# First batch of a split-weight two-layer kernel: the first layer in quarters instead of halves, with the weight decode put in the order of the quarters

## The chip, the cores and the metric

One core of one Trainium2 chip runs the kernel. The metric is device time in microseconds of one execution; three runs of the kernel before gave a median of 1534.24 us (1533.52 to 1536.03).

## What is computed

A packed attention (32 learned queries `p` per head attend to 576 keys, then the 576 queries attend to the 32 packed rows), then two feed-forward layers, all in float32; the weights come as float64 and are read as pairs of 32-bit words.

```python
def sm_attn(qq, kk, vv):
    s = scale * np.matmul(qq, kk.transpose(0, 1, 3, 2))
    a = np.exp(s - np.max(s, axis=-1, keepdims=True))
    return np.matmul(a / (np.sum(a, axis=-1, keepdims=True) + 1e-09), vv)
...
p_packed = sm_attn(p, k, v)                  # batch 8, heads 8, seq 576, head_dim 64, 32 packed rows
out = sm_attn(q, p_packed, p_packed)         # becomes x, 4608 tokens x 512
...
h = x @ w_in;  sp = log1p(exp(h));  x = (h * tanh(sp)) @ w_out     # layer 1, d_ff 2048
h = x @ w_in2; x = (h - tanh(h)) @ w_out2                          # layer 2, d_ff 2048
```

## The kernel before

All work is written down as operations with an engine, an estimated duration, dependences, buffers to take and give, and a **key**. `Plan.emit` walks a model of the machine and, whenever an engine is free, emits the ready operation with the lowest key whose buffers are free. So the keys set the order of each engine's queue; the queues then run in that order on the chip. `ka(n)` (L285) is the planned time of round `n` of layer 1.

**Layer 1** has 128 rounds `n` (`layer1`, L627): batch `b = n // 16`, half `hf` of its tokens (288 of 576), and pair `pr` of 128-wide feature columns. A round does on PE 12 matmuls of the first product (L641: two columns, two contractions, three high/low passes), on ACT two Mish (L645) and a rounding copy (L647), on DVE the low part (L648), and on PE 24 matmuls of the second product (L659) into four PSUM accumulators `acc`, which are evacuated when all 16 columns are summed (L670). In a batch the order is half 0 with pairs 0 to 7, then half 1 with pairs 0 to 7. So the first half of batch 0 needs every weight of layer 1.

**The weight decode.** `dec_unit` (L295) loads 512 KB of words into one of four buffers `st`, and builds float32 from them: on ACT a scale (L311) and for some units a second one (L314), on DVE otherwise L316, and always L318 and L321. The 16 units of the input weights, `w1i`, go to `xw` and `x` buffers (L356), are used by `mix` and stored to DRAM as `w1i_d` for the later batches (L365). The 16 units of the output weights, `w1o`, go through one scratch buffer `rr` (L326) and are split into high and low parts in `wo[i]` by ACT (L332) and DVE (L334). `unit_key` (L346) sets their order: four of `w1i`, four of `w1o`, and so on, all ahead of or within the first eight rounds.

**Attention** of a batch (`attention`, L441): scores (L479), maxima (L485), exponentials (L494), transposes (L506, L508), the packed product (L527, L535, L537); then for each half the second scores (L553) and a softmax on DVE and ACT (L558 to L580) that ends in `a2[b, hf]`, the input of L641. The exponential and Mish are in different ACT tables, and each change of table is an ACT_TABLE_LOAD. `mix` (L591) multiplies the packed rows into four `w1i` units (L609, evacuated by L615 and L617); four of them serve a batch. All loads and stores stand in SP's queue (L292). The second layer's weights are decoded in the same way during layer 1 (`dec_pair`, L370), and layer 2 (`pair2`, L740) follows. The `x` pool has ten buffers, shared by the loads of attention and the decode.

Of the kernel before, what the change touches and what calls it, by code (L numbers as in the profile page):

```python
# [21 lines left out]
HALF = S // 2  # L22
# [48 lines left out]
class Plan:  # L71
# [24 lines left out]
    def emit(self):  # L96
# [5 lines left out]
        table = None  # L102
# [111 lines left out]
def tile_packed_attention_mish_tanhshrink(  # L214
# [80 lines left out]
    def dec_unit(src, key, out, take, on_act, split=False, after=()):  # L295
# [6 lines left out]
        ld = dma(lambda: st.tile, lambda: src.bitcast(U32), 512, key - 10, take=[st])  # L302
# [7 lines left out]

        a = op("ACT", a_cost(512), lambda: A.activation(  # L311
# [8 lines left out]
        lds.append(ld)  # L320
# [4 lines left out]
    def dec_split(src, key, buf, view, on_act, scratch=False):  # L325
        w = Buf(K["rr"], [128, 512]) if scratch else buf  # L326
# [24 lines left out]
    unit = 0  # L351
    for g in range(4):
        for i in range(4 * g, 4 * g + 4):
            key = unit_key(unit)
            unit += 1
            buf = Buf(K["xw" if i < 6 else "x"], [128, 512 if i < 6 else 576])  # L356
            wt[0, i] = (buf, dec_unit(w1i[i], key, lambda b=buf: b.tile[:, :512], [buf], i >= 5))
        for i in range(4 * g, 4 * g + 4):
            key = unit_key(unit)
            unit += 1  # L360
            wo[i] = Buf(K["wo"], [128, 2, 512])
            wo_rd[i] = dec_split(w1o[i], key, wo[i], v_oc, True, True)
    for i in range(16):
        late = lds[min(31, 30 + i)]
        wt_st[i] = dma(lambda i=i: w1i_d[i], lambda b=wt[0, i][0]: b.tile[:, :512], 256, -46.8 + i,  # L365
                       [wt[0, i][1], late], give=[wt[0, i][0]])
# [74 lines left out]
    def attention(b):  # L441
# [15 lines left out]
        def load(src, n, kb_, key):  # L457
# [8 lines left out]
                   (k0 + 0.5 * (spans[0][1] - spans[0][0]) if b else -80.7) + i) for i in range(5)]  # L466
# [4 lines left out]
        def scores(j):  # L471
# [11 lines left out]
            s1 = op("PE", 1.19, f, key(2), [pt_ld] + [x[1] for x in kk], sc + [a1], [pt] + [x[0] for x in kk])  # L483
# [12 lines left out]
            ex = [op("ACT", 2 * a_cost(HALF, True, True) + 0.5, fe, key(2), [m], [sm] if j == 0 else [],  # L496
# [43 lines left out]
        def second_scores(hf):  # L540
            k0 = key()
            qq = [load(qT[b, i, :, hf * HALF:(hf + 1) * HALF], (128, HALF), 144, (k0 if b or hf else -57.94) + i)
# [48 lines left out]
    def mix(b, g):  # L591
        k0 = ka(16 * (b - 1) + 10 + 2 * g) if b else unit_key(8 * g + 3) - 52.37
# [3 lines left out]
        for c in range(4):  # L596
            i = 4 * g + c
            if b == 0:
                ws.append(wt[0, i])
            else:  # L600
                buf = Buf(K["xw"], [128, 512])
                ws.append((buf, dma(lambda buf=buf: buf.tile[:, :512], lambda i=i: w1i_d[i], 256,
                                    k0 - 12, [wt_st[i]], [buf])))
        pm = [bank(K["cap_s"]), bank(K["cap_s"])]

        def f():
            for j in range(2):
# [19 lines left out]
    def layer1(n):  # L627
        b, hf, pr = n // 16, n // 8 % 2, n % 8
        k0 = ka(n)
        kf = k0 - 4.87  # L630
        e, gt = Buf(K["e"], [128, 2, HALF]), Buf(K["g"], [128, 2, 2, HALF])
# [18 lines left out]
        for c in range(2):  # L650
            fc = 2 * pr + c
            for oc in range(4):
                if fc == 0:
# [3 lines left out]
                def f(c=c, oc=oc, fc=fc, ac=ac):  # L657
                    for i, (wl, gl) in enumerate(PASSES):
                        T.matmul(ac.tile[:, :HALF], r(wo[fc].tile[:, wl, oc * 128:(oc + 1) * 128]),  # L659
                                 r(gt.tile[:, gl, c, :]), start=(fc == 0 and i == 0), stop=(fc == NFC - 1 and i == 2))  # L660
# [250 lines left out]
```

## Time and profile before

| | us |
|---|---|
| median of three runs | 1534.24 |
| the profiled execution, device time | 1539.05 |
| its span, first to last instruction | 1536.9 |
| PE busy | 1494.9 |
| DVE busy | 1039.5 |
| ACT busy | 1007.6 |
| DMA, mean over the span | 189 GB/s |

The page gives busy time by engine, the span in 40 slices, the chain of work that ended last, and groups of instructions by source line. Views of the trace used below: the timeline (start, duration, what ended the idle time before), busy time by stretch (with the granted TensorE clock), and the chain.

### The profile page before, as it was taken

What the parts mean: (1) busy time and instruction counts of PE and PEld (TensorE: products, weight loads), DVE (VectorE), ACT (ScalarE), POOL (GpSimd) and SP (SyncE); (2) the same over time, 40 slices, a digit from 0 to 9 for tenths busy, and PEclk for the clock granted to TensorE, in tenths of its full rate; (3) what the DMA queues carried; (4) which work ended last, traced back from release to release, by engine and by line L of the source; (5) the groups of instructions that cost most, each with busy time, mean ns of one, the idle gap of its engine ahead of it and who ended that gap; (6) DMA issues with size and microseconds to landing.
All of it is one profiled execution on the core that took longest, in us unless ns stands there. A gap on an engine that the chain in (4) does not pass through costs nothing.

```text
span 1536.9 us, 28140 instructions
## 1 busy us (share of the span) xinstructions
PE 1494.9 (97%) x11112; PEld 1342.6 (87%) x11112; DVE 1039.5 (68%) x1905; ACT 1007.6 (66%) x1995; POOL 0.2 (0%) x4
## 2 busy tenths in 40 slices
PE   5599999999999999999999999999999999999999
PEld 1398989899898989899989898989989898989887
DVE  5955574563756543241378879897888889798876
ACT  5867765665666654553477767676776767676765
POOL 0000000000000000000000000000000000000000
PEclk9799999999999999999999999999999999999999
DMA  8676674481856443120975656566566656565561
GB/s 284 209 265 208 225 237 173 157 298 59 291 181 223 136 148 102 55 71 30 333 244 173 224 185 226 169 205 208 196 200 202 208 172 223 182 228 169 186 197 57
DMA packets 100084, 289.73 MB, mean 189 GB/s; under 512 B 10224, under 2 KB 27760, under 8 KB 90736
## 3 DMA queue, kind: packets, MB, share of 16 engines
q1 hardware_dynamic: 99952, 287.94, 56.0%
q8 instruction: 87, 1.43, 0.4%
q14 instruction: 45, 0.37, 0.1%
HBM read 241.76 MB, written 46.14 MB: 187 GB/s over the span
## 4 chain that ended last, share of the span: by engine, by line
PE 95%; DMA 2%; DVE 1%; ACT 1%; SPq 0%; issue 0%; DVEq 0%
PE acc L659 27%; PE acc L827 26%; PE bk L761 23%; PE bk L641 13%; PE bk L609 2%; PE bk L479 1%; PE bk L527 1%; PE bk L553 1%; DMA x<-in_v 1%; DMA m<-w2i_d 1%; DMA st<-in_w1o 0%; PE bk L506 0%; DMA x<-in_q 0%; DMA x<-in_k 0%; ACT st L311 0%
## 5 line engine op out<-in xcount | busy, mean ns | idle before, releaser
L827 PE MATMUL acc<-g,wo 128*128 128x512 f32 x1728 | 444.2, 393 | 0.0
L659 PE MATMUL acc<-g,wo 128*128 128x288 f32 x3072 | 438.2, 297 | 0.0
L659 PEld LDWEIGHTS acc<-g,wo 128*128 128x128 f32 x3072 | 416.1, 189 | 17.2 <-issue 16.6
L827 PEld LDWEIGHTS acc<-g,wo 128*128 128x128 f32 x1728 | 306.7, 189 | 50.1
L761 PEld LDWEIGHTS bk<-yh,m 128*128 128x128 f32 x2160 | 291.9, 191 | 20.7 <-DVE x L775 2.7
L761 PE MATMUL bk<-yh,m 128*128 128x256 f32 x2160 | 306.2, 284 | 0.1
L648 DVE TENSOR_TENSOR g<-e,g 128x576 fp32r<-128x576 f32 x128 | 96.7, 755 | 220.2 <-ACT g L647 214.0
L641 PEld LDWEIGHTS bk<-a,m 128*128 128x128 f32 x1536 | 212.4, 190 | 30.8 <-issue 8.4
L641 PE MATMUL bk<-a,m 128*128 128x288 f32 x1536 | 231.3, 300 | 5.9 <-ACT a L579 4.3
L645 ACT ACTIVATE e<-bk 128x288 f32<-128x288 f32 x256 | 103.3, 411 | 150.4 <-PE bk L641 149.5
L812 DVE TENSOR_TENSOR tt<-x,tt 128x512 f32<-128x512 f32 x144 | 99.3, 690 | 69.6 <-ACT tt L805 69.5
L801 ACT ACTIVATE e<-x 128x512 f32<-128x512 f32 x144 | 90.7, 630 | 70.6 <-DVE x L775 69.2
L772 ACT ACTIVATE pc<-bk 128x256 f32<-128x256 f32 x216 | 75.6, 374 | 70.0 <-PE bk L761 68.8
L761 PEld LDWEIGHTS bk<-a,m 128*128 128x128 f32 x864 | 113.3, 191 | 8.9 <-DMA m<-w2i_d 3.0
L761 PE MATMUL bk<-a,m 128*128 128x256 f32 x864 | 115.5, 283 | 2.8 <-DMA m<-w2i_d 2.8
L806 DVE SCALAR_TENSOR_TENSOR xw<-xw,xw 128x512 f32<-128x512 f32 x144 | 99.4, 690 | 26.0 <-ACT xw L804 24.3
L814 DVE COPY_PREDICATED xw<-e,tt 128x512 f32<-128x512 uint32 x144 | 109.6, 761 | 1.6
L775 DVE TENSOR_TENSOR x<-bk,pc 128x256 f32<-128x256 f32 x216 | 89.9, 417 | 23.3 <-PE bk L761 23.0
L816 ACT ACTIVATE g<-xw 128x512 fp32r<-128x512 f32 x144 | 89.3, 620 | 22.9 <-DVE xw L814 22.4
L817 DVE TENSOR_TENSOR g<-xw,g 128x512 fp32r<-128x512 f32 x144 | 98.8, 686 | 6.9 <-ACT g L816 6.8
L802 ACT ACTIVATE xw<-e,c_qb 128x512 f32<-128x512 f32 x144 | 102.2, 710 | 0.0
L810 DVE SCALAR_TENSOR_TENSOR xw<-xw,x 128x512 f32<-128x512 f32 x144 | 98.6, 685 | 0.0
(94 smaller groups left out, 1264.1 us busy)
## 6 DMA issues: line engine op xcount, KB each, us to landing
m<-w2i_d SPq DMA_DIRECT2D x72, 1024.0 KB, 5.1
m<-w2i_d SPq DMA_DIRECT2D x72, 768.0 KB, 4.4
xw<-w1i_d SPq DMA_DIRECT2D x112, 256.0 KB, 4.3
w2i_d<-x SPq DMA_DIRECT2D x56, 256.0 KB, 3.7
x<-in_k SPq DMA_DIRECT2D x32, 288.0 KB, 4.8
x<-in_q SPq DMA_DIRECT2D x64, 144.0 KB, 4.0
y_d<-yv SPq DMA_DIRECT2D x16, 576.0 KB, 3.9
out_t<-x SPq DMA_DIRECT2D x36, 256.0 KB, 5.1
```

The lines of the kernel that those rows point to most:

```text
L641: T.matmul(h.tile[:, :HALF], r(m.tile[:, fc % 4, kc, wl, :]), r(x.tile[:, kc, al, :]), start=(i == 0), stop=(i == 5))
L645: fr.append(op("ACT", a_cost(HALF, True), lambda c=c, h=h: A.activation(e.tile[:, c, :], h.tile[:, :HALF], AF.Mish), kf + 1, [g1] + fr, [e ...
L648: lo = op("DVE", v_cost(576), lambda: V.tensor_tensor(out=r(gt.tile[:, 1]), in0=e.tile, in1=gt.tile[:, 0], op=ALU.subtract), kf + 1.2, [hi ...
L659: T.matmul(ac.tile[:, :HALF], r(wo[fc].tile[:, wl, oc * 128:(oc + 1) * 128]), r(gt.tile[:, gl, c, :]), start=(fc == 0 and i == 0), stop=(f ...
L761: T.matmul(bk.tile[:, :HB], r(wv[:, kc, wl, :]), r(yq[blk, j].tile[:, kc, yl, :]), start=(first and i == 0), stop=(i == 5), skip_group_che ...
L802: p1 = op("ACT", a_cost(TB, False, True), lambda: A.activation(s1.tile, zz.tile, AF.Sigmoid, bias=c_qb, scale=Q_L), k0 + 0.1, [sq], [s1])
L806: q = op("DVE", v_cost(TB), lambda: V.scalar_tensor_tensor(out=s1.tile, in0=s1.tile, scalar=Q_E, in1=s2.tile, op0=ALU.add, op1=ALU.mult), ...
L810: q = op("DVE", v_cost(TB), lambda: V.scalar_tensor_tensor(out=s1.tile, in0=s1.tile, scalar=Q_A, in1=h.tile, op0=ALU.mult, op1=ALU.mult), ...
L812: d = op("DVE", v_cost(TB), lambda: V.tensor_tensor(out=tt.tile, in0=h.tile, in1=tt.tile, op=ALU.subtract), k0 + 1.3, [th], give=[h])
L814: q = op("DVE", v_cost(TB), lambda: V.copy_predicated(s1.tile, zz.tile.bitcast(U32), tt.tile), k0 + 1.4, [q, d, k], give=[zz, tt])
L817: lo = op("DVE", v_cost(TB), lambda: V.tensor_tensor(out=r(gt.tile[:, 1, :]), in0=s1.tile, in1=gt.tile[:, 0, :], op=ALU.subtract), k0 + 2. ...
L827: T.matmul(ac.tile, r(w2c[fc].tile[:, wl, oc * 128:(oc + 1) * 128]), r(gt.tile[:, gl, :]), start=(fc == 0 and i == 0), stop=(fc == NFC - 1 ...
```

## The change

Batch 0 goes through layer 1 in four quarters: half 0 with pairs 0 to 3, half 1 with pairs 0 to 3, half 0 with pairs 4 to 7, half 1 with pairs 4 to 7 (`place`). The sums of the first two quarters are copied from PSUM by ACT into `part` (two `x` buffers a half), and DVE adds them to the sums of the other two quarters, in place of ACT's last copy. The decode keys follow the quarters (`w1i_key`, `w1o_key`), `w1o` uses two scratch buffers in turn (`rr` and the second layer's `so`), four `w1i` units are decoded into `wo` buffers, the first four `w1i` loads and the values `v` are issued early, and the second scores' `q` loads and the attention of batch 1 get other keys. The buffer of the first exponentials is taken by the exponential and no longer by the scores. Batches 1 to 7 and layer 2 keep their order.

```diff
-    def dec_split(src, key, buf, view, on_act, scratch=False):
-        w = Buf(K["rr"], [128, 512]) if scratch else buf
+    def dec_split(src, key, buf, view, on_act, scratch=None):
+        w = Buf(K[scratch], [128, 512]) if scratch else buf
...
-    def unit_key(u):
-        i = u // 8 * 4 + u % 4
-        return -83.7 + 3.72 * i if u % 8 < 4 else -79.34 + 6.62 * i
+    def place(hf, pr):
+        return pr // 4 * 8 + hf * 4 + pr % 4
+
+    def w1i_key(i):
+        return ka(place(0, i // 4 * 2)) - 7.0 - 1.2 * (4 - i % 4) - (0 if i < 4 else 6.0)
+
+    def w1o_key(i):
+        return ka(place(0, i // 2) + 2) - 9.0 + 3.0 * (i % 2) - (0 if i < 8 else 6.0)
...
+        kd = "wo" if 4 <= i < 8 else "x" if i > 13 else "xw"
...
+        wt[0, i] = (buf, dec_unit(w1i[i], key, wv, [buf], i % 4 > 1, early=-190.5 + i if i < 4 else None), wv)
+        wo[i] = Buf(K["wo"], [128, 2, 512])
+        wo_rd[i] = dec_split(w1o[i], w1o_key(i), wo[i], v_oc, True, "rr" if i % 2 == 0 else "so")
...
-        wt_st[i] = dma(lambda i=i: w1i_d[i], lambda b=wt[0, i][0]: b.tile[:, :512], 256, -46.8 + i,
+        wt_st[i] = dma(lambda i=i: w1i_d[i], wv, 256, w1i_key(i) + 25, [dec, lds[9 if i < 8 else 29]], give=[buf])
...
-            spans = [(ka(16 * b - 16) + 20.02 + (15.83 if b == 1 else 0), ka(16 * b - 8) + 8.64, 26)]
-            spans += [(ka(16 * b + 8 * hf - 8) - 13.96, ka(16 * b + 8 * hf) - 21.81, 14) for hf in range(2)]
+            spans = [(ka(8.5), ka(12.5), 26) if b == 1 else (ka(16 * b - 16) + 20.02, ka(16 * b - 8) + 8.64, 26)]
+            spans += [(ka(16 * b + 8 * hf - 8) - 13.96, ka(16 * b + 8 * hf) - 21.81, 14) if b > 1 else
+                      (ka(12 + 2 * hf), ka(14.5 + 2.5 * hf), 14) for hf in range(2)]
...
-            spans = [(-200.0, -180.0, 26), (-180.0, -170.0, 14), (-170.0, -160.0, 14)]
+            spans = [(-200.0, -180.0, 26), (-180.0, -170.0, 14), (ka(0.5), ka(2.5), 14)]
...
-                   (k0 + 0.5 * (spans[0][1] - spans[0][0]) if b else -80.7) + i) for i in range(5)]
+                   (k0 + 0.5 * (spans[0][1] - spans[0][0]) if b else -176.0) + i) for i in range(5)]
...
-        k0 = ka(n)
+        k0 = ka(n if b else place(hf, pr))
+        first, last = (0, NFC - 1) if b else (pr // 4 * 8, pr // 4 * 8 + 7)
...
                 if fc < NFC - 1:
+                    if oc % 2 == 0:
+                        part[hf, oc // 2] = Buf(K["x"], [128, 2, HALF])
+                    p = part[hf, oc // 2]
+                    part_rd[hf, oc] = op("ACT", a_cost(HALF, True), lambda ac=ac, oc=oc, p=p: A.activation(
+                        p.tile[:, oc % 2, :], ac.tile[:, :HALF], AF.Copy), k0 + TA,
...
+                if b == 0:
+                    p = part[hf, oc // 2]
+                    yvops.append(op("DVE", v_cost(HALF), lambda ac=ac, oc=oc, yv=yv, p=p: V.tensor_tensor(
+                        out=yv.tile[:, oc, :], in0=ac.tile[:, :HALF], in1=p.tile[:, oc % 2, :], op=ALU.add), k0 + TA,
```

Three places show what this does to the queues. In the changed kernel most lines are numbered a few higher: L318, L334, L479, L494, L579, L580, L609, L617, L641, L645, L648, L659 are L319, L334, L484, L499, L584, L585, L614, L622, L648, L652, L655, L666 there.

**DVE, up to the first `a2`** (`a_0`, written by L580 before and L585 after). Before:

```order
L318 SCALAR_TENSOR_TENSOR x_378<-st_343,x_378 128x512
L576 TENSOR_TENSOR ex_328<-ex_328,s_0_376 128x576
L617 TENSOR_TENSOR m_361<-bk_359,m_361 128x4x128
L578 STREAM_TRANSPOSE fx_329<-ex_328 128x576
L617 TENSOR_TENSOR m_361<-bk_360,m_361 128x4x128
L334 TENSOR_TENSOR wo_386<-rr_356,wo_386 128x512
L580 TENSOR_TENSOR a_0_330<-fx_329,a_0_330 128x2x288
```

After the change:

```order
L334 TENSOR_TENSOR wo_338<-rr_305,wo_338 128x512
L581 TENSOR_TENSOR ex_271<-ex_271,s_0_336 128x576
L321 SCALAR_TENSOR_TENSOR so_316<-st_282,so_316 128x512
L583 STREAM_TRANSPOSE fx_272<-ex_271 128x576
L622 TENSOR_TENSOR m_322<-bk_320,m_322 128x4x128
L334 TENSOR_TENSOR wo_358<-so_316,wo_358 128x512
L585 TENSOR_TENSOR a_0_273<-fx_272,a_0_273 128x2x288
```

Before, 64 DVE instructions stand ahead of that write: 15 of L318, 14 of L321, 5 of L316, 5 of L334, 4 of L617 among them. After, 50 do: 10, 10, 4, 2 and 3; the other 21 are the same.

**PE, the first rounds** (`a_0` and `a_1` are the two halves of batch 0, `bk` a PSUM bank, `m` a mix). Before:

```order
L641 MATMUL bk_457<-a_0_330,m_296 128x288 x6
L641 MATMUL bk_466<-a_0_330,m_296 128x288 x6
L641 MATMUL bk_478<-a_0_330,m_361 128x288 x6
L609 MATMUL bk_533<-x_349,ppb_228 32x512
L609 MATMUL bk_533<-x_378,ppb_228 32x512
L609 MATMUL bk_533<-x_397,ppb_228 32x512
```

After the change:

```order
L648 MATMUL bk_423<-a_0_273,m_295 128x288 x6
L648 MATMUL bk_432<-a_0_273,m_295 128x288 x6
L648 MATMUL bk_445<-a_0_273,m_322 128x288 x6
L648 MATMUL bk_457<-a_0_273,m_322 128x288 x6
L666 MATMUL acc_0_467<-g_417,wo_338 128x288 x3
L666 MATMUL acc_0_473<-g_417,wo_338 128x288 x3
```

The third mix stood in PE's queue ahead of every second product, and the fourth right behind the first three of these matmuls; now the two stand behind the first products of rounds 6 and 8.

**ACT, ahead of batch 1's first exponentials** (`a_0` here is their buffer). Before:

```order
L645 ACTIVATE e_1131<-bk_1117 128x288
L645 ACTIVATE e_1131<-bk_1124 128x288
L647 ACTIVATE g_1140<-e_1131 128x576
L311 ACTIVATE st_1009<-st_1009 128x512
L311 ACTIVATE st_1029<-st_1029 128x512
L494 ACT_TABLE_LOAD
L494 ACTIVATE a_0_1160,sm_1190<-bk_1158,mx_1176 128x288
```

After the change:

```order
L678 ACTIVATE x_978<-acc_0_728 128x288
L652 ACTIVATE e_994<-bk_980 128x288
L315 ACTIVATE rr_1000<-st_920 128x512
L312 ACTIVATE st_940<-st_940 128x512
L332 ACTIVATE wo_1022<-so_972 128x512
L652 ACTIVATE e_994<-bk_1003 128x288
L499 ACT_TABLE_LOAD
L499 ACTIVATE a_0_1031,sm_1032<-bk_905,mx_935 128x288
```

The decode of `w1o` 10 to 12 and the copies of the partial sums now stand among the Mish ahead of these exponentials; before, the decode of the first layer was over by then.

## Rows read from the trace of the kernel before

**Rows 1.** The page, busy time of PE over the span.

```profile
PE 1494.9 (97%) x11112; PEld 1342.6 (87%) x11112; DVE 1039.5 (68%) x1905; ACT 1007.6 (66%) x1995; POOL 0.2 (0%) x4
```

**Rows 2.** Stretches: length, then busy us (instructions) of PE, PEld, DVE, ACT, POOL, clock, DMA share, GB/s.

```profile
40.00:60.00 20.00, 9.46 (x56) 6.04 (x56) 19.60 (x36) 16.35 (x27) 0.00 (x0) 0.97 0.69 219
60.00:80.00 20.00, 16.32 (x84) 10.11 (x85) 16.23 (x26) 17.77 (x34) 0.00 (x0) 0.60 0.64 188
```

**Rows 3.** Timeline of PE: start, length, line, count, [idle before, ended by].

```profile
48.96 3.01 PE L641 MATMUL bk<-a,m 128*128 128x288 f32 x11 [0.51 <-DVE a L580]
52.36 3.05 PE L641 MATMUL bk<-a,m 128*128 128x288 f32 x18 [0.39 <-DVE ex L558]
63.03 1.93 PE L609 MATMUL bk<-x,ppb 64*32 64x512 f32 x8 [7.62 <-ACT e L645]
72.87 4.47 PE L659 MATMUL acc<-g,wo 128*128 128x288 f32 x21
```

**Rows 4.** The same view as rows 2, around the return of the clock.

```profile
60.00:76.00 16.00, 12.31 (x54) 6.11 (x55) 15.16 (x25) 15.17 (x29) 0.00 (x0) 0.50 0.68 201
76.00:80.00 4.00, 4.00 (x32) 4.00 (x32) 1.07 (x2) 2.60 (x5) 0.00 (x0) 1.00 0.49 134
```

**Rows 5.** Stretch to batch 1's first product, first products (L641) alone.

```profile
0.00:150.40 150.40, 31.53 (x192) 28.24 (x192) 0.94 0.74 241
```

**Rows 6.** The same stretch, second products (L659) alone.

```profile
0.00:150.40 150.40, 51.40 (x345) 48.42 (x345) 0.94 0.74 241
```

**Rows 7.** The same stretch, mixes (L609, 16 records each) alone.

```profile
0.00:150.40 150.40, 14.78 (x96) 1.92 (x96) 0.94 0.74 241
```

**Rows 8.** The chain that ended last: start, length, what, count.

```profile
86.89 1.59 PE bk L641 x12
88.48 3.18 PE acc L659 x24
119.49 1.10 PE bk L479 x16
125.56 0.44 PE bk L506 x4
135.89 1.66 PE bk L527 x80
139.45 0.65 PE bk L553 x16
152.66 1.02 PE bk L609 x16
```

**Rows 9.** Groups by line and shape, first 300 us, DVE: busy us, mean ns.

```profile
L617 DVE TENSOR_TENSOR m<-bk,m 128x512 fp32r<-128x512 f32 x26 | 16.8, 679 | 0.4 <-ACT m L615 0.4
L321 DVE SCALAR_TENSOR_TENSOR rr<-st,rr 128x512 uint32<-128x512 uint32 x16 | 11.0, 687 | 0.2
L318 DVE SCALAR_TENSOR_TENSOR rr<-st,rr 128x512 uint32<-128x512 uint32 x16 | 11.0, 684 | 6.5 <-ACT rr L314 6.5
L334 DVE TENSOR_TENSOR wo<-rr,wo 128x512 fp32r<-128x512 f32 x16 | 10.9, 684 | 6.2 <-ACT wo L332 6.2
L316 DVE TENSOR_SCALAR xw<-st 128x512 uint32<-128x512 uint32 x5 | 2.1, 423 | 1.3 <-DMA st<-in_w1i 1.3
```

**Rows 10.** Timeline of DVE: the first `a2`, and the first low part of a round.

```profile
48.16 0.74 DVE L580 TENSOR_TENSOR a<-fx,a 128x576 fp32r<-128x576 f32 x1
65.46 0.75 DVE L648 TENSOR_TENSOR g<-e,g 128x576 fp32r<-128x576 f32 x1
```

**Rows 11.** Groups by line and shape, first 165 us, ACT: busy, mean | idle before, ended by.

```profile
L645 ACT ACTIVATE e<-bk 128x288 f32<-128x288 f32 x38 | 15.3, 409 | 12.5 <-PE bk L641 12.2
L670 ACT ACTIVATE yv<-acc 128x288 f32<-128x288 f32 x8 | 3.1, 419 | 0.9 <-PE acc L659 0.8
```

**Rows 12.** Timeline of DVE: decode of three `w1o` units while PE is full, first and last.

```profile
81.52 0.69 DVE L321 SCALAR_TENSOR_TENSOR rr<-st,rr 128x512 uint32<-128x512 uint32 x1
91.07 0.69 DVE L321 SCALAR_TENSOR_TENSOR rr<-st,rr 128x512 uint32<-128x512 uint32 x1
```

More of the change, by code (lines that the diff above doesn't have):

```diff
@@ L101, in emit @@
         dma_free, changes, failed = 0.0, 0, {}
-        table = None
+        table = "exp"
         warm, seen, busy = False, 0, {}
@@ L292, in dma, with dec_unit @@
         return op("SP", kbytes / 350.0, lambda: SP.dma_start(out(), in_()), key, deps, take, give)
-    def dec_unit(src, key, out, take, on_act, split=False, after=()):
+    def dec_unit(src, key, out, take, on_act, split=False, after=(), early=None):
         st = Buf(K["st"], [128, 1024], U32)
-        ld = dma(lambda: st.tile, lambda: src.bitcast(U32), 512, key - 10, take=[st])
+        ld = dma(lambda: st.tile, lambda: src.bitcast(U32), 512, key - 10 if early is None else early, take=[st])
         def w(i):
@@ L591, in mix @@
     def mix(b, g):
-        k0 = ka(16 * (b - 1) + 10 + 2 * g) if b else unit_key(8 * g + 3) - 52.37
+        k0 = ka(16 * (b - 1) + 10 + 2 * g) if b else ka(place(0, 2 * g)) - 6.0
         m = mt[b, g] = Buf(K["m"], [128, 4, 2, 2, 128])
@@ L652, in layer1 @@
             for oc in range(4):
-                if fc == 0:
+                if fc == first:
                     acc1[oc] = Buf(K["acc", oc], [128, 512])
@@ L659, in f @@
                         T.matmul(ac.tile[:, :HALF], r(wo[fc].tile[:, wl, oc * 128:(oc + 1) * 128]),
-                                 r(gt.tile[:, gl, c, :]), start=(fc == 0 and i == 0), stop=(fc == NFC - 1 and i == 2))
+                                 r(gt.tile[:, gl, c, :]), start=(fc == first and i == 0), stop=(fc == last and i == 2))
                 prev = g2_last.get(oc)
                 g2_last[oc] = z = op("PE", 0.37, f, k0 + 2.62 * TA + 0.1 * (4 * c + oc), [lo, wo_rd[fc], prev],
-                                     [ac] if fc == 0 else [], [gt] + ([wo[fc]] if n >= NA - 8 else []))
+                                     [ac] if fc == first else [], [gt] + ([wo[fc]] if n >= NA - 8 else []))
+                if fc < last:
+                    continue
                 if fc < NFC - 1:
+                    if oc % 2 == 0:
[3 more added lines that the diff above has]
+                        p.tile[:, oc % 2, :], ac.tile[:, :HALF], AF.Copy), k0 + TA,
+                        [z] + ([part_rd[hf, oc - 1]] if oc % 2 else []), [p] if oc % 2 == 0 else [], [ac])
                     continue
@@ L679, in tile_packed_attention_mish_tanhshrink @@
     acc1, yv_, yvops = {}, [None], []
+    part, part_rd = {}, {}
     w2c, w2c_rd = {}, {}
@@ L849, in tile_packed_attention_mish_tanhshrink @@
             mix(b, g)
-    for n in range(NA):
+    for n in sorted(range(NA), key=lambda n: (n // 16, n % 16 if n > 15 else place(n // 8, n % 8))):
         layer1(n)
```

40 lines of the change are left out of this document (17 added, 23 removed).

## The prediction

> **What bounds the kernel now.** I read the page first: PE is busy for 97% of the span [rows 1], so the kernel can only get faster where PE stands still, or where its busy time is not work at full pace. The stretches show where that is. Between 40 and 60 us PE is busy for 9.46 of 20 us, while DVE is busy for 19.60 and ACT for 16.35 [rows 2]: these two decode weights, and PE waits for them. The timeline of PE shows the waits. The first product starts at 48.96, as soon as DVE has written the first `a2`; eighteen more follow at 52.36; then PE has nothing until a Mish at the end of ACT's queue frees a bank at 63.03, 7.62 us later [rows 3]. The first round's low part, which the first second product needs, comes on DVE only at 65.46 [rows 10]. During that gap the granted clock falls to 0.50, that is from 2.4 to 1.2 GHz, and it is back only at 76 [rows 4]. From then on PE is full.
>
> To put one number on the start, I count what PE has done when batch 1 begins at 150.4 us. It is 192 first products, 345 second products and six mixes (96 records) [rows 5 to 7], and the PE part of two attentions. At full pace 12 first products take 1.59 us and 24 second ones 3.18, so 0.1325 each; a mix takes 1.02; an attention takes 2 x 1.10 + 2 x 0.44 + 1.66 + 2 x 0.65 = 6.0 [rows 8], and some 0.3 for its small transposes, an estimate from the row of 0.44. That makes 537 x 0.1325 + 6 x 1.02 + 2 x 6.3 = 89.9 us. So **60.5 of the first 150.4 us are lost**, and the change can win a part of them. Behind batch 1's start the order of PE is nearly the same before and after, and PE is full; what is won at that point should stay won.
>
> **The change, part by part.**
>
> *The first `a2`.* Its last step, at 48.16 us [rows 10], stands on DVE behind 64 instructions before and behind 50 after. Fourteen decode steps move behind it: five L318, four L321, one L316, three L334, one L617, at 0.684, 0.687, 0.423, 0.684 and 0.679 [rows 9], 9.3 us together. DVE is full there [rows 2], so the first product moves from 48.96 to **39.6**. The bounds: not earlier at all, if the loads set the pace (SP now issues four `w1i` and all `v` loads ahead of `q`); 12 us earlier, if dropping the wait for the late `v` adds to it. I take DVE's sum, as DVE's share is the row nearest to the place.
>
> *The first two quarters.* From there PE does 168 matmuls until it has finished round 3 and has the first products of rounds 4 and 5, and in between the second scores of the other half (0.65). That is 22.3 + 0.65 us at full pace. The first matmuls after a wait are slower: eleven took 3.01 us, 0.274 each [rows 3]. If only twelve are so slow this adds 1.7 us, if all 36 before the first second product are, 5.1; I take 4.5, since the second scores stand between them as the gap did before. PE is then at this point at 39.6 + 22.3 + 0.65 + 4.5 = **67.0 us**. What it needs is there: the second half's `a2` stands 29 DVE instructions behind the first, the last `wo` of the first quarter 37; at 20 us for 36 [rows 2] they come at about 56 and 61, and PE asks for the first at 60. This cover is 4 us; without it the wait takes its place.
>
> By the trace this slow start is paid once. The Trainium skill (TensorE: Matmul & The Clock Gate, HAM oscillation) says that a kernel whose bursts of matmuls are parted by waits pays it in each burst, and that speaks against this change, which moves new waits between batch 0 and batch 1 (below); taken so, the sum would come out as in the second rival.
>
> *The second half of the decode.* Sixteen units, two mixes and batch 1's attention now run beside full rounds, and PE's queue is strict about batch 1: behind its transposes of the first exponentials stand rounds 9 to 11. ACT is the late one. It ends the `wo` that PE needs for round 3 at about 64, just behind the Mish of round 5, and 51 instructions later come the exponentials. When pressed ACT did 29 instructions in 16 us [rows 4], 0.552 each, so 28.1 us; nine of the 51 are Mish, whose waits for PE average 12.5 / 38 = 0.33 [rows 11], so 3.0 more: 95.1. PE has 168 matmuls, a mix and one score step until then: 67.0 + 22.3 + 1.0 + 1.1 = 91.4. It waits **3.7 us**. The second exponentials are 24 instructions further on ACT, six of them Mish: 13.2 + 2.0, so 110.3; PE needs 78 matmuls, one score step and transposes, 12.0 us, and is there at 107.1: **3.2 us**. Together 6.9; the bounds are 0 (ACT fills its waits with decode) and twice as much.
>
> *Small things.* The partial sums add eight ACT copies (0.419 each [rows 11]), and eight DVE adds replace eight such copies. I cost them at nothing: the twelve first products that stand between the last sum of a quarter and the next quarter cover a copy with 1.6 us. Without that cover the four copies cost 1.7 us at each of the two new borders. The third and fourth partial sums of half 1 need `x` buffers that batch 1's keys hold; this falls into the same wait. On SP no transfer is added. Eight stores of `w1i_d` move ahead of the loads of the last two `wo` of the first quarter; 2 MB at 219 GB/s [rows 2] is 9.6 us in the worst case. The time between hides this: their buffers come free four DVE instructions behind the first `a2`, at about 42, and DVE wants the words 28 behind it, at 56. Loads that came later than that would hold round 3 by as much.
>
> *The sum.* From 67.0 to the first product of batch 1 PE has 384 matmuls, five mixes, one attention and the waits: 67.0 + 50.9 + 5.1 + 6.3 + 6.9 = 136.2 us. It has then done 15 matmuls and one mix more than before at 150.4, worth 3.0 us, so this compares with 153.4. **The gain is 17.2 us.** The profiled execution took 1539.05 us in all, 4.8 over the median; the sum makes 1521.8 of it, and **1517.0** of the median.
>
> **The rivals.**
>
> *No new wait.* ACT and DVE keep ahead, as they do behind 76 before. Then the 6.9 us do not arise: 1510.1. For it speaks that each engine's sum fits; against it, that ACT has 108 instructions (60 us at 0.552) in 69 us, in order, with six table loads.
>
> *The clock falls again.* PE waits twice near the exponentials, and the clock goes to 0.50 as it did in the gap before 63. That spell held 12.31 us of busy PE [rows 4], half of it lost: 6.2 us each, two make 12.3, so 1529.3. Against it: the falling took a gap of 7.62 us in the rows, and my waits are 3 to 4. By the rule named above this happens; of shorter waits no row of this kernel tells.
>
> *The second half of the decode becomes the bound, and the kernel is slower.* While PE was full, DVE finished one `wo` unit in (91.07 - 81.52) / 2 = 4.78 us [rows 12], one a round. If the sixteen late units also come at that pace, they end at 64.7 + 76.5 = 141.2; PE needs the last one for round 11, at 67.0 + 36.6 + 2.0 + 4.9 + 6.9 = 117.4. It is 23.8 us late: 1540.8, slower by 6.6. The case decides from 4.37 us a unit, where the lateness eats the 17.2. For it speaks ACT's load; against it, that the pace in those rows is that of a written order with one unit a round, one scratch buffer, and engines with time to spare: pressed, between 40 and 60, ACT and DVE did 27 and 36 instructions in 20 us [rows 2], and a unit needs at most three on either, 1.7 us of DVE or 2.2 of ACT.
>
> **How the numbers follow.** The forecast gets 0.68, no new wait 0.12, the lost clock 0.10, the late decode 0.10. The forecast's own bounds (waits from 0 to twice, a slow start of 1.7 to 5.1, a first `a2` some microseconds off) reach from 1508 to 1527; this also takes in the first rival and leaves out the other two. No change that can be told is a difference within 0.2%, 3.1 us, about what a measurement of this kernel can tell. Faster by more than that are the forecast, the first rival and most of the second: 0.88. Between: 0.03. Slower: 0.09.
>
> **What would show it.** The first product should start near 40 us, PE's gap of 7.62 us and the half clock up to 76 should be gone, and the first product of batch 1 should start near 136. ACT should end PE's longest waits between 90 and 112, at the transposes of batch 1. I am wrong if the first product comes after 45, if PE waits for DVE's `wo` after 80, or if the clock shows 0.50 behind 70 us.

## The result and the profile after

The changed kernel takes **1516.34 us** (median of four runs, 1515.54 to 1519.44); the kernel before took 1534.57 beside it. The ratio is 0.988, 95% interval 0.9868 to 0.9892, so 18.2 us are gone. The profiled execution took 1519.44 us, 19.6 less than that of before, with TensorE busy for 1485.4 us in place of 1494.9 [rows 1].

Busy time by stretch, the changed kernel (columns as in [rows 2]); the two short stretches show when the clock comes up:

```profile
40.00:60.00 20.00, 19.82 (x140) 18.62 (x141) 19.17 (x34) 18.33 (x32) 0.00 (x0) 0.85 0.58 210
60.00:80.00 20.00, 20.00 (x160) 19.00 (x159) 17.20 (x29) 16.42 (x35) 0.00 (x0) 1.00 0.86 290
80.00:100.00 20.00, 18.24 (x151) 14.56 (x150) 15.66 (x30) 18.56 (x39) 0.00 (x0) 1.00 0.79 276
...
120.00:140.00 20.00, 19.54 (x169) 14.96 (x168) 16.75 (x35) 13.48 (x25) 0.00 (x0) 1.00 0.87 293
...
44.00:46.00 2.00, 2.00 (x15) 1.74 (x8) 1.81 (x4) 2.00 (x5) 0.00 (x0) 0.52 1.03 371
46.00:48.00 2.00, 2.00 (x17) 2.00 (x16) 2.00 (x4) 1.80 (x5) 0.00 (x0) 1.00 0.91 350
```

Between 40 and 60 us DVE is about as busy as it was (19.17 us for 19.60) and ACT a little more (18.33 for 16.35), but TensorE now works beside them for 19.82 us in place of 9.46. The granted clock is at 1.00 from 46 us on; before, it showed 0.50 from 60 to 76 [rows 4].

Timeline of PE, the changed kernel (columns as in [rows 3]; L648, L666 and L614 are the first product, the second product and the mix, L511 the transposes of the exponentials):

```profile
40.19 3.01 PE L648 MATMUL bk<-a,m 128*128 128x288 f32 x11 [0.21 <-DVE a L585]
...
59.02 1.74 PE L648 MATMUL bk<-a,m 128*128 128x288 f32 x12
...
62.58 3.34 PE L666 MATMUL acc<-g,wo 128*128 128x288 f32 x24
65.76 1.75 PE L648 MATMUL bk<-a,m 128*128 128x288 f32 x12
...
86.74 1.05 PE L648 MATMUL bk<-a,m 128*128 128x288 f32 x6 [0.38 <-DVE m L622]
...
88.92 1.85 PE L648 MATMUL bk<-a,m 128*128 128x288 f32 x12 [0.33 <-ACT e L652]
...
94.63 1.72 PE L666 MATMUL acc<-g,wo 128*128 128x288 f32 x11 [0.40 <-DVE g L655]
...
98.01 1.07 PE L648 MATMUL bk<-a,m 128*128 128x288 f32 x6 [0.56 <-ACT a1T L515]
...
106.86 0.60 PE L511 MATMUL bk<-ident,a 128*128 128x128 f32 x4
...
123.87 2.50 PE L614 MATMUL bk<-xw,ppb 64*32 64x512 f32 x16
...
134.69 1.49 PE L648 MATMUL bk<-a,m 128*128 128x288 f32 x9 [0.46 <-DVE m L622]
```

The eleven first products start at 40.19 in place of 48.96 [rows 3], 8.8 us earlier. Batch 1 starts at 134.69. PE has then done 552 dense matmuls, seven mixes and two attentions, which the prediction's unit times price at 73.1 + 7.1 + 12.6 = 92.9 us: 41.8 us are lost where 60.5 were. Of the 18.7 us won there, 8.8 lie ahead of the first products and 9.9 behind them, where the gap of 7.62 us was. Behind batch 1's start nothing of it is given back: from there to the end of the span are 1382.9 us, and before they were 1383.5 (1536.9 - 150.41 - 3.0, for the 15 matmuls and the mix that are still to do there).

### The profile page after: what moved, and what is told of

The parts are those of the page before. It is cut to its first block, busy times and chain, and to the rows that moved or that the text cites. A ratio compares the mean times of both kernels' runs of the same rounds, so it can differ in the third digit from the quotient of the medians.

```text
span 1517.6 us, 28157 instructions
## 1 busy us (share of the span) xinstructions
PE 1485.4 (98%) x11112; PEld 1340.3 (88%) x11112; DVE 1044.0 (69%) x1916; ACT 1003.6 (66%) x1992; POOL 0.2 (0%) x4
## 4 chain that ended last, share of the span: by engine, by line
PE 94%; DMA 3%; ACT 2%; DVE 1%; issue 0%; SPq 0%; ACTq 0%
PE acc L850 26%; PE acc L666 26%; PE bk L784 24%; PE bk L648 14%; PE bk L614 2%; PE bk L484 1%; DMA st<-in_w1i 1%; PE bk L532 1%; DMA st<-in_w1o 1%; PE bk L558 1%; DMA x<-in_v 1%; DMA m<-w2i_d 1%; PE bk L511 0%; DMA xw<-w1i_d 0%; ACT st L312 0%
## 5 line engine op out<-in xcount | busy, mean ns | idle before, releaser
L666 PE MATMUL acc<-g,wo 128*128 128x288 f32 x3072 | 436.6, 296 | 0.4 <-DVE g L655 0.4
L666 PEld LDWEIGHTS acc<-g,wo 128*128 128x128 f32 x3072 | 414.3, 188 | 16.1 <-issue 14.6
L648 PEld LDWEIGHTS bk<-a,m 128*128 128x128 f32 x1536 | 212.4, 190 | 35.7 <-ACT a L584 9.4
L648 PE MATMUL bk<-a,m 128*128 128x288 f32 x1536 | 231.2, 300 | 10.5 <-ACT a L584 8.5
L655 DVE TENSOR_TENSOR g<-e,g 128x576 fp32r<-128x576 f32 x128 | 96.6, 755 | 202.7 <-ACT g L654 196.4
L652 ACT ACTIVATE e<-bk 128x288 f32<-128x288 f32 x256 | 103.4, 411 | 140.6 <-PE bk L648 139.9
L829 DVE SCALAR_TENSOR_TENSOR xw<-xw,xw 128x512 f32<-128x512 f32 x144 | 99.4, 690 | 25.6 <-ACT xw L827 23.9
```

The costliest lines, as they stand in the source:

```text
L648: T.matmul(h.tile[:, :HALF], r(m.tile[:, fc % 4, kc, wl, :]), r(x.tile[:, kc, al, :]), start=(i == 0), stop=(i == 5))
L652: fr.append(op("ACT", a_cost(HALF, True), lambda c=c, h=h: A.activation(e.tile[:, c, :], h.tile[:, :HALF], AF.Mish), kf + 1, [g1] + fr, [e ...
L655: lo = op("DVE", v_cost(576), lambda: V.tensor_tensor(out=r(gt.tile[:, 1]), in0=e.tile, in1=gt.tile[:, 0], op=ALU.subtract), kf + 1.2, [hi ...
L829: q = op("DVE", v_cost(TB), lambda: V.scalar_tensor_tensor(out=s1.tile, in0=s1.tile, scalar=Q_E, in1=s2.tile, op0=ALU.add, op1=ALU.mult), ...
```

## Experiments

For the traces I use one yardstick: the time from the eleven first products to batch 1's first product, brought to the 552 dense matmuls and seven mixes of the changed kernel (0.1325 a matmul, 1.02 a mix). It is **94.5 us** in the changed kernel (134.69 - 40.19) and 104.4 before (150.41 - 48.96 + 3.0). It leaves out how early the first product comes, which differs by up to 1.7 us between profiled executions whose programs are the same up to there (48.96 in the kernel before, and 48.08, 47.94 and 47.25 in three runs below that edit it further on).

**The decode's order without the quarters.** The changed kernel, batch 0 in halves again, without partial sums. The keys of the decode are written in terms of the rounds, so they follow the halves here; the early loads and the two scratch buffers stay:

```diff
     def place(hf, pr):
-        return pr // 4 * 8 + hf * 4 + pr % 4
+        return hf * 8 + pr
...
-        first, last = (0, NFC - 1) if b else (pr // 4 * 8, pr // 4 * 8 + 7)
+        first, last = 0, NFC - 1
...
-                if b == 0:
+                if False:
```

> The changed kernel with batch 0 in halves again (half 0 through all eight pairs, then half 1; no partial sums); the decode keys, written in terms of the rounds, the loads and the two scratch buffers stay. Theory (the quarters halve what must be decoded per round, and the start itself comes from the decode order): the first product stays near 39 us, since the same 50 DVE instructions stand ahead of it, but PE must wait for output-weight units between 65 and 110 us, because sixteen units are wanted in some 38 us; 1526 to 1531 us. Rival (the decode order alone makes the gain, the quarters nothing): 1516 to 1519 us, no wait of PE for a decoded weight.

Measured: 1530.14 us, ratio 0.997 (0.996 to 0.998). Timeline of PE in this kernel, then its stretch from 60 to 80 us:

```profile
38.10 3.01 PE L648 MATMUL bk<-a,m 128*128 128x288 f32 x11 [0.21 <-DVE a L585]
...
60.79 0.85 PE L666 MATMUL acc<-g,wo 128*128 128x288 f32 x2 [1.27 <-ACT wo L332]
...
75.31 2.14 PE L666 MATMUL acc<-g,wo 128*128 128x288 f32 x6 [5.86 <-ACT wo L332]
```

```profile
60.00:80.00 20.00, 13.07 (x73) 10.24 (x74) 17.17 (x29) 15.14 (x29) 0.00 (x0) 0.76 0.87 292
```

The early first product is there, and most of it is given back to waits for `wo`, since the first half still asks for every weight, and the clock falls in them. The decode's order without the quarters is worth about 4.5 us (3 to 6 by the interval).

**The quarters without the decode's order.** The kernel before with `place`, the partial sums and batch 1's attention keys of the change; decode, scratch and loads stay. The two lines that make the quarters:

```diff
-        k0 = ka(n)
+        k0 = ka(n if b else place(hf, pr))
...
+        first, last = (0, NFC - 1) if b else (pr // 4 * 8, pr // 4 * 8 + 7)
```

> The kernel before with the order of rounds in quarters and the partial sums, and batch 1's attention keys of the change (without them the order can't be planned); decode order, scratch buffer and loads of batch 0 as before. The first 94 rows of PE's queue are then those of the kernel before. Theory (the quarters pay only through the decode order that they allow): first product at 49 us, the gap before 63 us and the half clock up to 76 us are still there, 1532 to 1537 us. Rival (the order of rounds by itself makes a good part of the gain): 1527 us or less.

Measured: 1536.68 us, ratio 1.0011 (1.0 to 1.0021): nothing won. Timeline of PE:

```profile
47.38 3.01 PE L647 MATMUL bk<-a,m 128*128 128x288 f32 x11 [0.52 <-DVE a L584]
...
61.46 1.93 PE L613 MATMUL bk<-x,ppb 64*32 64x512 f32 x8 [6.93 <-ACT e L651]
```

The late first product and the gap of before are both there. So the two parts alone bring about 4.5 and nothing, and together 18: the quarters halve what TensorE asks for early, and the order of the decode has to deliver just that half.

**One scratch buffer.** The changed kernel with all of `w1o` through `rr`:

```diff
-        wo_rd[i] = dec_split(w1o[i], w1o_key(i), wo[i], v_oc, True, "rr" if i % 2 == 0 else "so")
+        wo_rd[i] = dec_split(w1o[i], w1o_key(i), wo[i], v_oc, True, "rr")
```

> The changed kernel with all output-weight units through one scratch buffer (rr), as before. Theory (ACT's and DVE's whole queues set the pace, not the chain through one buffer): 1516 to 1519 us, first product within 1 us of 39.4. Rival (the second scratch buffer is what lets the late decode keep up; with one, a unit takes 4 to 5 us as in the kernel before): PE waits for decoded weights behind 50 us, 1522 us or more.

Measured: 1523.84 us, ratio 0.9935 (0.992 to 0.995). My theory fell. The rival's time held, though of TensorE's waits only the last of these lines names a decoded `wo`. The yardstick is 99.2 us (98.82, with three matmuls fewer), 4.7 more than in the changed kernel. Waits of PE from 30 to 110 us, but for the one ahead of the first product (us in total, times, longest):

```profile
PE acc L666 <- ACT x L678: 1.4, 2, 0.8
PE bk L648 <- DVE m L622: 1.3, 2, 1.0
PE bk L648 <- DVE a L585: 1.3, 2, 1.1
PE acc L666 <- ACT wo L332: 0.8, 1, 0.8
```

Behind these stands the chain inside a unit, which I had left out when I counted instructions on each engine: with one scratch the next unit may not begin before DVE has done L334 of the last. In the same stretch DVE waits 6.8 us for ACT to fill `rr` (L315), and ACT 3.4 us for DVE's L321 on it and 1.2 us for DVE's L334 to free it; in the changed kernel the three waits are 0.2, 0.4 and 0.2 us. The second buffer, which the prediction named as a difference of the two kernels but gave no term, is worth 4.7 us by the yardstick and 7.5 by the medians; which is nearer stays open.

**The old load keys.** The changed kernel with the loads of `w1i` 0 to 3, `v` and `q` keyed as before:

```diff
-        wt[0, i] = (buf, dec_unit(w1i[i], key, wv, [buf], i % 4 > 1, early=-190.5 + i if i < 4 else None), wv)
+        wt[0, i] = (buf, dec_unit(w1i[i], key, wv, [buf], i % 4 > 1), wv)
...
-                   (k0 + 0.5 * (spans[0][1] - spans[0][0]) if b else -176.0) + i) for i in range(5)]
+                   (k0 + 0.5 * (spans[0][1] - spans[0][0]) if b else -80.7) + i) for i in range(5)]
...
-            qq = [load(qT[b, i, :, hf * HALF:(hf + 1) * HALF], (128, HALF), 144, (k0 if b else -169.0 + 150 * hf) + i)
+            qq = [load(qT[b, i, :, hf * HALF:(hf + 1) * HALF], (128, HALF), 144, (k0 if b or hf else -57.94) + i)
```

> The changed kernel with the old load keys in batch 0: the first four input-weight loads, the v loads and the q loads as in the kernel before. Theory (DVE's order sets the first product): first product at 39 to 42 us, 1516 to 1519 us. Rival (v and the first weights arriving earlier is what moved the first product): first product at 45 us or later, 1522 us or more.

Measured: 1516.96 us, ratio 0.9884 (0.9868 to 0.9901); the yardstick is 94.4. Timeline of PE:

```profile
39.14 3.01 PE L648 MATMUL bk<-a,m 128*128 128x288 f32 x11 [0.21 <-DVE a L585]
```

The early loads are worth nothing here. What is left is the order of the decode: the first products come early in every run that keeps it (38.10 in halves, 38.86 with one scratch buffer, 39.14 here) and late in the one that does not (47.38, the quarters alone).

**The price of the half clock.** The kernel before with extra matmuls in TensorE's gap ahead of 63 us, their results unread:

```diff
+                if n == 2 and fc == 4:
+                    for _ in range(40):
+                        T.matmul(h.tile[:, HALF:512], r(m.tile[:, fc % 4, 0, 0, :]), r(x.tile[:, 0, 0, :512 - HALF]),
+                                 start=True, stop=True)
```

In a first try (e5_fill_gap) the condition was written with a loop variable that has another value by the time the function is called, so no extra matmul was in the program:

> The kernel before, and in TensorE's gap of 7.62 us ahead of 63 us forty extra matmuls of 224 columns, written to unused columns of a bank, so that the order of everything else stays. It prices the half clock by itself. My theory (the price in the second rival of the prediction): before, 12.31 us of busy TensorE between 60 and 76 us ran at 0.50 and half of that, 6.2 us, is lost to the clock; if the clock stays at 1.00 behind 60 us the kernel takes 1528 to 1531 us. Rival: TensorE is paced by ACT and DVE there anyway, the clock column goes to 1.00 and the time stays within 1533 to 1537. If the clock still shows 0.50 behind the gap, the run tells nothing of either.

Measured: 1535.78 us, ratio 0.9996 (0.9987 to 1.0006), which shows what a repeat of the same program gives. Its yardstick is 104.4 (149.50 - 48.08 + 3.0), that of the kernel before once more, and 104.5 in the next run, so the yardstick repeats to about 0.1 us. With the edit above (e9_fill_gap2):

> The kernel before with forty extra matmuls of 224 columns on TensorE behind the last first product that runs ahead of the gap of 7.62 us, written to unused columns of the same bank; nothing else moves (in the run called e5_fill_gap this edit did not take, no extra matmul stood in its program, so that one is a plain repeat of the kernel before). It prices the half clock by itself. My theory, the price in the second rival of the prediction: before, 12.31 us of busy TensorE between 60 and 76 us ran at 0.50, and half of that, 6.2 us, is lost to the clock; if the clock stays at 1.00 behind 60 us the kernel takes 1528 to 1532 us. Rival: TensorE is paced by ACT and DVE there anyway, the clock column goes to 1.00 and the time stays within 1533 to 1537. A third: the extra matmuls last longer than the gap and hold what comes behind, over 1537. If the clock still shows 0.50 behind the gap, the run tells nothing of the first two.

Measured: 1535.32 us, ratio 0.9999 (0.999 to 1.0008). Timeline of PE, and a stretch behind the gap:

```profile
54.24 4.62 PE L646 MATMUL bk<-a,m 128*128 128x224 f32 x40
62.05 1.93 PE L609 MATMUL bk<-x,ppb 64*32 64x512 f32 x8 [3.19 <-ACT e L649]
```

```profile
65.00:70.00 5.00, 5.00 (x25) 2.38 (x17) 4.63 (x9) 5.00 (x12) 0.00 (x0) 0.50 0.68 234
```

The clock fell within this wait of 3.19 us: it read 1.00 from 50 to 60 us, 0.85 from 60 to 62 and 0.50 from 62 to 74. So this run tells nothing of the price. With 66 in place of 40:

> As the run e9_fill_gap2, with 66 extra matmuls in place of 40. Forty took 4.62 us and left a wait of 3.19, and the clock fell to 0.50 all the same; 66 take 7.6 us and leave about 0.2, so what remains ahead of the full work behind 69 us is a wait of 0.65 between two halves of a mix. If the clock stays at 1.00 behind 60 us: my theory (half of 12.31 us of busy TensorE is lost to the clock) says 1528 to 1532, the rival (TensorE is paced by ACT and DVE there) 1533 to 1537. If it falls again, short waits and sparse work are enough for it to fall, the time is that of the kernel before, and the price of the half clock is left to the rows.

Measured: 1536.20 us (1532.88 to 1539.60, eleven runs), ratio 1.0009 (1.0 to 1.0019). Timeline of PE in the profiled execution, which was the fastest of the eleven:

```profile
61.53 1.06 PE L609 MATMUL bk<-x,ppb 64*32 64x512 f32 x8
64.01 1.06 PE L609 MATMUL bk<-x,ppb 64*32 64x512 f32 x8 [1.41 <-ACT e L649]
65.94 1.43 PE L641 MATMUL bk<-a,m 128*128 128x288 f32 x6 [0.87 <-ACT e L649]
...
70.59 3.05 PE L663 MATMUL acc<-g,wo 128*128 128x288 f32 x21
```

And, beside [rows 3], the second half of that mix in the kernel before:

```profile
65.61 1.93 PE L609 MATMUL bk<-x,ppb 64*32 64x512 f32 x8 [0.65 <-ACT e L645]
```

The 21 second products take 3.05 us in place of 4.47 [rows 3], and each group of eight mix records 1.06 in place of 1.93, but the waits for ACT's Mish grow from 0.65 to 1.41 and 0.87. The yardstick goes from 104.4 to 102.4 (146.67 - 47.25 + 3.0). The clock read 1.00 behind 55 us but for 66 to 70, at 0.61 and 0.54. So to have it up for most of this stretch is worth **2.0 us, not the 6.2** that I had taken from half of 12.31 us. Of the 4.2 between them 1.6 went into the grown waits for ACT (1.41 + 0.87 - 0.65), and some 1.7 may still be lost in the 4.0 us that ran at 0.61 and 0.54 (an estimate: the missing share of the clock times these 4.0 us). In the median nothing shows; whether the other ten executions kept the clock is open.

**Batch 1's attention one round later or earlier.** The changed kernel with one pair of keys moved:

```diff
-            spans = [(ka(8.5), ka(12.5), 26) if b == 1 else (ka(16 * b - 16) + 20.02, ka(16 * b - 8) + 8.64, 26)]
+            spans = [(ka(9.5), ka(13.5), 26) if b == 1 else (ka(16 * b - 16) + 20.02, ka(16 * b - 8) + 8.64, 26)]
```

> The changed kernel with the keys of batch 1's first scores, exponentials and packed product one round later (ka(9.5) to ka(13.5)). The first exponentials stand 33 instructions later in ACT's queue, and TensorE asks for them after 522 matmuls of layer 1 in place of 336, the score steps and mixes after them are crowded into the last 54 before batch 1. Theory (the wait of 3.6 us near 98 us is ACT's exponentials queued behind the decode): this wait goes, but the attention's own chain (exponential, packed product, mix, second scores, softmax) has no cover left ahead of batch 1's first product, and TensorE waits there 6 to 10 us: 1518 to 1524 us, with no wait at the first exponentials. Rival (the decode itself is late and TensorE waits for it near 98 us whatever stands in between): the wait near 98 us stays, with wo in place of a1T as its releaser, and the time is over 1522 us by both waits. Third: the cover is enough, 1512 to 1514 us.

Measured: 1524.87 us, ratio 0.9924 (0.9908 to 0.9941). Timeline of PE:

```profile
116.63 0.60 PE L511 MATMUL bk<-ident,a 128*128 128x128 f32 x4
...
137.09 1.91 PE L614 MATMUL bk<-xw,ppb 64*32 64x512 f32 x7 [3.10 <-DMA xw<-w1i_d]
...
149.69 0.53 PE L648 MATMUL bk<-a,m 128*128 128x288 f32 x2 [3.17 <-DVE m L622]
```

No wait is left at the exponentials, PE is busy for 20.00 of 20 us from 80 to 100, and the cover is gone where batch 1 begins, as the theory had it; the time is 0.9 us over its range. The mixes wait there for the reloads of `w1i_d`, a releaser I had not named. Then `ka(7.5), ka(11.5)`:

> The changed kernel with the same keys one round earlier (ka(7.5) to ka(11.5)). The first exponentials stand 14 instructions earlier in ACT's queue (7.7 us at 0.552), and TensorE asks for them 24 matmuls earlier (3.2 us); the second ones 12 earlier (6.6 us), asked for 69 matmuls earlier (9.1 us). Theory (ACT's queue sets the wait near 98 us): the 3.6 us go, the second exponentials cost up to 2.5 us: 1513 to 1517 us. Rival (the loads of p and k, which now stand further ahead of the w1o loads, or the decode that is put off, hold TensorE at a later round): over 1518 us, with wo or m as the releaser.

Measured: 1519.75 us, ratio 0.9893 (0.9877 to 0.9909). Timeline of PE and two stretches:

```profile
90.67 1.83 PE L484 MATMUL bk<-x,x 64*32 64x288 f32 x16 [1.25 <-ACT a1T L515]
92.42 3.25 PE L648 MATMUL bk<-a,m 128*128 128x288 f32 x12
```

```profile
90.00:92.00 2.00, 1.33 (x16) 0.35 (x16) 2.00 (x4) 2.00 (x6) 0.00 (x0) 0.79 0.31 55
92.00:94.00 2.00, 2.00 (x13) 1.58 (x7) 2.00 (x6) 2.00 (x5) 0.00 (x0) 0.50 0.71 243
```

Neither theory: TensorE's named waits from 66 us on are shorter (1.5 us in all, 2.1 in the changed kernel), but around the one of 1.25 us, among sparse transposes and scores, the clock falls, and it reads 0.50 until 98. The yardstick is 96.2 (93.06, with 24 matmuls fewer), 1.7 over the changed kernel.

**Second scores early.** The changed kernel with the second scores of half 1 keyed as before:

```diff
-            spans = [(-200.0, -180.0, 26), (-180.0, -170.0, 14), (ka(0.5), ka(2.5), 14)]
+            spans = [(-200.0, -180.0, 26), (-180.0, -170.0, 14), (-170.0, -160.0, 14)]
```

> The changed kernel with the second scores and softmax of half 1 of batch 0 at the key of the kernel before, ahead of the first rounds. The second a2 is written 6 DVE instructions earlier, the first one at the same place. TensorE has no wait there in the changed kernel (20.0 of 20 us busy from 60 to 80, 19.82 from 40 to 60), so both theories that I can think of say little: within 2 us of the changed kernel, 1514 to 1518 us, if the cover at that place is enough either way; over 1519 us if the softmax pushes the first quarter's last wo, which stood 2 us ahead of its use, behind it.

Measured: 1520.12 us, ratio 0.9895 (0.9873 to 0.9918); the yardstick is 96.8 (93.66, with 24 fewer). The time is that of the second case, but the releaser is not its `wo`: PE waits early for the first rounds' `g`, behind the softmax, and is busy for 18.19 us between 40 and 60 in place of 19.82:

```profile
48.45 0.40 PE L666 MATMUL acc<-g,wo 128*128 128x288 f32 x1 [0.94 <-ACT g L654]
49.33 3.32 PE L666 MATMUL acc<-g,wo 128*128 128x288 f32 x23 [0.48 <-DVE g L655]
```

**ACT relieved** (e10_copies_on_dve). The changed kernel with the partial sums copied by DVE:

```diff
-                    part_rd[hf, oc] = op("ACT", a_cost(HALF, True), lambda ac=ac, oc=oc, p=p: A.activation(
-                        p.tile[:, oc % 2, :], ac.tile[:, :HALF], AF.Copy), k0 + TA,
+                    part_rd[hf, oc] = op("DVE", v_cost(HALF), lambda ac=ac, oc=oc, p=p: V.tensor_copy(
+                        p.tile[:, oc % 2, :], ac.tile[:, :HALF]), k0 + TA,
```

> The changed kernel with the eight partial sums copied from PSUM by DVE in place of ACT; the planner then also has batch 1's first exponentials 9 instructions earlier in ACT's queue (116 ahead of them in place of 125), while TensorE asks for them after the same 336 matmuls. Theory (ACT's queue alone sets the wait near 98 us; the part of the prediction that charged ACT with 51 instructions there): nine instructions at 0.552 are 5.0 us, more than the 3.6 us lost between 66 and 98, so these go: 1512 to 1514 us. Rival (the loads of w1o set ACT's pace there: its one wait in that stretch was for such a load, and DVE's copies hold the buffers that the loads want): ACT waits for loads by as much as it saved, TensorE's loss between 66 and 98 us stays at 3 us or more, 1515 us and over.

Measured: 1518.11 us, ratio 0.9894 (0.9878 to 0.9909), no gain over the changed kernel. The yardstick is 94.1 (94.48, with three matmuls more), 0.4 better. PE has no wait for a1T any more, so ACT's queue did set that one. The theory's 1512 to 1514 is missed and the rival's time holds, but its mechanism is not there either: ACT waits 1.6 us for loads between 66 and 100, against 1.4. But the time came back as a wait at batch 1's start. The chain that leads to it, on ACT, DVE and PE of this kernel:

```profile
121.43 0.68 ACT L312 ACTIVATE st<-st 128x512 f32<-128x512 f32 x1 [3.71 <-DMA st<-in_w2i]
122.13 1.28 ACT L575 ACT_TABLE_LOAD   x1
```

```profile
124.14 0.75 DVE L576 TENSOR_REDUCE s<-ex 128x18 f32<-128x576 f32 x1 [3.10 <-ACT ex L575]
```

```profile
133.45 2.81 PE L648 MATMUL bk<-a,m 128*128 128x288 f32 x19 [1.71 <-DVE m L622]
```

A decode step of the second layer, whose load is late, stands on ACT ahead of the softmax's exponential (L575). In the changed kernel the same step waits 2.52 us:

```profile
122.07 0.67 ACT L312 ACTIVATE st<-st 128x512 f32<-128x512 f32 x1 [2.52 <-DMA st<-in_w2i]
```

**That step behind the softmax.** The last kernel, with the fifth and sixth L312 of the second layer's weights made to follow that exponential:

```diff
+        if split:
+            late.append(a)
...
+            if b == 1 and hf == 0:
+                for x in late[4:6]:
+                    z.outs.append(x)
+                    x.wait += 1
```

> The kernel of e10_copies_on_dve with one more edit: ACT's scale step (L312) of the fifth and sixth unit of the second layer's input weights is put behind the exponential of batch 1's first softmax. In e10 ACT stood 3.71 us in such a step, waiting for the load (ended 121.4 us), with that exponential next in its queue; DVE's sum waited 3.10 us for it, and TensorE then 1.71 us for m at batch 1's first product. Theory (that load holds the softmax and with it batch 1): ACT's wait ahead of the exponential is gone, the first product of batch 1 follows the kernel's first product after 93 to 94 us in place of 95.3, and the time is 1514 to 1516.5 us. Rival (the mixes ahead of batch 1 are late by their own loads of w1i_d, whatever the softmax does): the wait for m stays at 1.5 us or more, and the time is within 1.5 us of e10, 1516.5 to 1519.5 us.

Measured: 1516.50 us, ratio 0.9877 (0.9858 to 0.9895). ACT and PE (the lines are seven higher; L655 is the first product):

```profile
121.03 0.69 ACT L578 ACTIVATE ex<-ex 128x576 f32<-128x576 f32 x1 [1.03 <-DVE ex L576]
```

```profile
133.10 1.85 PE L655 MATMUL bk<-a,m 128*128 128x288 f32 x12 [0.42 <-DVE m L629]
```

The wait for the load is gone, that for `m` falls from 1.71 to 0.42, and batch 1's first product follows the kernel's first one (38.78) after 94.3 us, a little over the 93 to 94 expected. The median lies where the ranges of the theory and the rival meet, so it is the waits that speak for the theory. Brought to 552 matmuls, the yardstick is 93.9 us, 0.6 under the changed kernel: too little for these intervals to tell. None of the versions tried is measurably faster than the changed kernel.

## Why the prediction was right

**The first product.** Forecast 39.6, measured 40.19. The run with the old load keys shows that the loads do not do it, and the runs in halves and with the quarters alone show that the order of the decode does.

**The first two quarters.** From there to the end of round 3's second products 27.4 us were forecast and 25.6 measured (65.76). The work in it was right; the slow start of TensorE, taken as 4.5 us, is what 22.3 + 0.65 leave of 25.6, some 2.7. The cover, forecast at 4 us for the second half's `a2`, was much thinner. DVE in the changed kernel:

```profile
57.28 0.75 DVE L585 TENSOR_TENSOR a<-fx,a 128x576 fp32r<-128x576 f32 x1
...
62.95 0.69 DVE L334 TENSOR_TENSOR wo<-so,wo 128x512 fp32r<-128x512 f32 x1 [0.23 <-ACT wo L332]
```

This `a2` is done at 58.03, and PE takes it up at 59.02; the quarter's last `wo` is done at 63.64, and PE wants it from about 64.2 (an estimate: half way through the 24 second products that start at 62.58). That even so much is left hangs on the second scratch buffer: with one, PE waits for both.

```profile
56.62 1.75 PE L648 MATMUL bk<-a,m 128*128 128x288 f32 x11 [1.12 <-DVE a L585]
...
68.92 0.53 PE L666 MATMUL acc<-g,wo 128*128 128x288 f32 x2 [0.77 <-ACT wo L332]
```

**The waits ahead of batch 1.** From 65.76 to 134.69 are 68.9 us, of which work is 62.3 (50.9 + 5.1 + 6.3): 6.6 us of waits, where 6.9 were forecast. The sum was right and its parts were not all, so that the two agree is in part luck. Up to 98.01 the loss is 3.6 us, beside the forecast's 3.7, but it is not one wait at the first transposes: 1.7 of it are four short waits (m, e, g and a1T, 0.33 to 0.56 each), and the rest is work a little slower than its unit times around them. ACT ends the longest of them, as the prediction's signs had it, but at the first product of 98.01 and not at the transposes. ACT began these exponentials at 92.1 and not 95.1. From 63.24 to 90.84 it did 47 instructions in 27.6 us, of which 4.3 are waits (3.0 for Mish, as forecast, and 1.4 for a load): 0.49 each, and not 0.552. The prediction also put one mix ahead of these transposes where two stand, which alone takes 1.0 from its 3.7.

The wait of 3.2 at the second exponentials did not come: the transposes at 106.86 run without one. ACT, which I had at 110.3 there, ended these exponentials at 106.1: the first ones came earlier, and it waited for nothing between the two, where I had charged 2.0. The other 2.5 us lie behind 117.77 instead, at the mix of 123.87, which takes 2.50 us in place of 1.02, and at the 0.46 for `m`. The weight loads of that mix wait for the reloads of `w1i_d` (waits from 100 to 136 us, both in this mix):

```profile
PEld bk L614 <- DMA xw<-w1i_d: 1.2, 2, 0.6
```

The step that failed is the count of ACT's instructions at 0.552 with Mish waits on top. For the reloads of `w1i_d` and for the softmax of batch 1 behind a late load the prediction had no term; what that late load costs in the changed kernel itself no run shows.

**The sum.** Batch 1's first product was forecast for 136.2 and came at 134.69; 17.2 us of gain were forecast, and 18.7 are there by the same count. The medians differ by 18.2.

**The rivals.** The late decode did not come: PE waits for no `wo` behind 66, and DVE is busy for 15.66 of 20 us from 80 to 100. The clock did not fall in the changed kernel, with 1.76 us of idle time in the 20 us that hold the waits; but with the keys one round earlier it did, and the yardstick there is 1.7 longer. So the second rival was nearer than its 0.10 said, and cheaper than its 12.3 us. The Trainium skill (TensorE: Matmul & The Clock Gate, HAM oscillation) has it that bursts of matmuls parted by waits, for DMA and of some 3 to 5 us in its case, pay the slow start each time. The trace of the changed kernel does not test that: between 46 us and batch 1 no wait of TensorE is longer than 0.56 us, and the clock stays at 1.00. In the run with the earlier attention it read 0.50 behind a wait of 1.25 us, which is shorter than those of the page's case.

**The part that was never priced alone.** The prediction did not say how much of its gain is the order and how much the quarters. The runs do: 4.5, nothing, and 18 together. The order of the decode is taken here with all that came with it. Two parts of it are not in the list of the change: three of the `w1i` units get their second scale on DVE in place of ACT (eleven units had it on ACT before, eight after), and the mixes of batch 0 have new keys. No run takes back these, the `w1i` units in `wo` buffers or the buffer of the first exponentials by themselves.

## What to carry to other kernels

Where a start-up is bound by preparing weights, splitting the first work so that it asks for half of them pays only if the preparation is put in that order too, and has the buffers to run ahead; try the parts apart before you keep either. To price a stretch at half clock, look at what else ends its waits: here 2.0 of the 6.2 us came back when most of the stretch ran at full clock, and 1.6 turned into waits for ACT. A load that is late costs the bound engine time when its consumer stands, in a strict queue, ahead of something that this engine needs.

## What was not expected of the hardware

The clock fell in much shorter waits than the 7.62 us of [rows 3]: in one of 3.19 us in one run, and around one of 1.25 us in another, where TensorE was busy for 2.41 of the 4 us from 88 to 92. And the first matmuls after a wait are slow under either reading of the clock: eleven first products took 3.01 us both in the kernel before, where the granted clock read 1.00 from 48 to 52 us, and in the changed one, where it read 0.50 from 40 to 44.
